# Storing outputs after the last load, moving weight loads, and transposing three more chunks by DMA in a fused recurrence and feed-forward kernel

## The chip, the core and the metric

One core of one Trainium2 chip. The metric is device microseconds of one execution. "Before" is the kernel that was tuned already; "after" is the changed one. A run is called slow when it lies over 1.5% above the fastest run of the same kernel, and ratios use the other runs alone.

## The reference

```python
f = 1 / (1 + exp(-f_logit))                    # q, k, v, f_logit: 4 x 8 x 768 x 48, float32
for t in range(768):
    state = f[:, :, t, :, None] * state + k[:, :, t] (outer) v[:, :, t]
    y[:, :, t] = q[:, :, t] @ state
x = y as 3072 tokens x 384
out = relu(x @ w_in) ** 2 @ w_out              # w_in 384 x 2048, w_out 2048 x 384
```

## The kernel before

The recurrence is worked in 24 chunks of 128 steps, 6 for each of the 4 batch entries; a chunk's result goes through the feed-forward part. A scheduler written in the kernel takes steps with planned durations and makes one static order for each engine. So TensorE, VectorE, ScalarE, GpSimd and SyncE each do their work in a fixed order, and wait in it. The parts that matter:

```python
LOADS = [0, "i0", 1, "i1", 2, "i2", 3, "i3", 4, "o0", "o1", 5, "o2", "o3"] + list(range(6, NCH))
XBAR = 14                                       # from this chunk on, DMA transposes q and k
...
def load(i):                                    # SyncE: f, k, q, v of chunk i, 192 KB each, 192-byte rows
    plan.add(f"{n}{i}", "SP", 0.45, fn, take=["io_" + n], rank=0, data=(1.07, 1024))
...
def load_w(kind, s, behind):                    # GpSimd: a quarter of w_in (i) or w_out (o), cast to bf16
    plan.add(f"cw{kind}{s}", "POOL", 1.0, fn, after=[f"vc.{behind}"], rank=-1, data=(2.4, 0))
for x in LOADS:
    if isinstance(x, int):
        load(x); chunk = x
    else:
        load_w(x[0], x[1], max(chunk - 1, 0))   # waits for the cast of v of that chunk
...
# a chunk: a1 (ScalarE, needs f) -> p1 (TensorE, prefix sum) -> exp -> v1k, v1q (VectorE, need k and q)
#   -> p2 (TensorE: 8 transposes, 4 need k, 4 need q), or one DMA transpose from chunk XBAR on
#   -> p3 -> p4 (needs v, the state); p5 -> s1 -> s2 (GpSimd: the next state)
...
soft = i < NCH - 6
def dma(i=i, soft=soft):                        # the store of a chunk's output
    (nc.gpsimd if soft else nc.sync).dma_start(out[i * C:(i + 1) * C, :], st["ob", i])
```

Fill matmuls on zeros are put where the scheduler expects TensorE to be idle in the first 40 us.

Of the kernel before, what the change touches and what calls it, by code (L numbers as in the profile page):

```python
# [9 lines left out]
F32 = mybir.dt.float32  # L10
# [12 lines left out]
class Planner:  # L23
# [27 lines left out]
    def order(self, fill=None, first=0.0, last=0.0, unit=0.11):  # L51
# [28 lines left out]
        moved_to, queue = 0.0, []  # L80
        while count < len(left):
            while gives and gives[0][0] <= t + 1e-9:
                given.add(heapq.heappop(gives)[1])
            moved = True
            while moved:
                moved = False
                for eng in list(ready):
                    group = ready[eng]
                    if avail.get(eng, 0.0) > t + 1e-9 or not group:
                        continue  # L90
                    best = None
                    for n, r in group.items():
                        s = left[n]
                        if r > t + 1e-9 or not can(s):
                            continue
                        d = s.ways[eng][0]
                        if any(max(avail.get(e, 0.0), t) + w[0] < t + d - 1e-9 for e, w in s.ways.items() if e != eng):
                            continue
                        key = (s.rank if s.rank is not None else r, seq[n])
                        if best is None or key < best[0]:  # L100
                            best = (key, n)
                    if best is None:
                        continue
                    n = best[1]
                    s = left[n]
                    for e in s.ways:
                        ready[e].pop(n, None)
                    for x in s.take:
                        taken[x].append(n)
                    dur, fn = s.ways[eng]  # L110
                    end = t + dur
                    if s.data:
                        us, size = s.data
                        while sum(z for e, z in queue if e > end) + size > self.RING:
                            end = min(e for e, z in queue if e > end)
                        moved_to = max(moved_to, end + self.FIRST) + us
                        queue.append((moved_to, size))
                    avail[eng] = end
                    ran[n] = (t, end, eng)
                    if fill and eng == "PE":  # L120
                        gap = t - max(busy, first) - 2 * unit
                        if gap > 0 and t < last:
                            res.append(lambda k=int(gap / unit) + 1: fill(k))
                        busy = end
                    res.append(fn)
                    count += 1
                    heapq.heappush(events, end)
                    fin = moved_to + self.RECEIPT if s.data else end + s.land
                    heapq.heappush(events, fin)
                    for x in s.give:  # L130
                        heapq.heappush(gives, (fin, tuple(x.split(":"))))
                    for u in users.get(n, ()):
                        waiting[u] -= 1
                        at = ready_at.setdefault(u, {e: 0.0 for e in left[u].ways})
                        for e in at:
                            at[e] = max(at[e], end if e == eng and s.land == self.LAT else fin)
                            heapq.heappush(events, at[e])
                        if waiting[u] == 0:
                            release(u, at)
                    moved = True  # L140
                    break
            while events and events[0] <= t + 1e-9:
                heapq.heappop(events)
            if count < len(left):
                assert events, ("stuck", [n for e in ready.values() for n in e][:20])
                t = events[0]
# [5 lines left out]
def kernel(  # L152
# [10 lines left out]
    nc = tc.nc  # L163
    B, H, S, D = q.shape
    assert (B, H, S, D) == (4, 8, 768, 48)
    C = 128
# [4 lines left out]
    d_model, d_ff = moe_w_in.shape  # L171
    assert d_model == HD
    KS = d_model // C
    FS = d_ff // C
    NCH = B * NC
    IOB = 7
    HTB = 3
    LOADS = [0, "i0", 1, "i1", 2, "i2", 3, "i3", 4, "o0", "o1", 5, "o2", "o3"] + list(range(6, NCH))
    LOADS = [x if isinstance(x, int) else (x[0], int(x[1])) for x in LOADS]
    FILL = 40.0  # L180
    XBAR = 14
    XBAR2 = 18
    UNITS = [(0, 2), (2, 1), (3, 1), (4, 1), (5, 1)] + [(c, 3) for c in range(6, NCH, 3)]

# [6 lines left out]
    ffp = ctx.enter_context(tc.tile_pool(name="ffp", bufs=2))  # L191
# [4 lines left out]

    plan = Planner()
    plan.buffers(**{"io_" + n: IOB for n in "fkqv"})
    plan.buffers(m=2, tr=1, at0=1, at1=1, h=2, o=1, hr=3, hT=HTB, xT=2, ob=4,
                pz=2, az=4, vz=4, ts=3, am=2, ys=3, ep=2, en=4)  # L200
    st = {}
    copy = {"ACT": nc.scalar.copy, "DVE": nc.vector.tensor_copy}
# [64 lines left out]
    def attention(i):  # L267
        c = i % NC
        last = c == NC - 1
        g, o = divmod(i, GC)  # L270
        rank = (i - 6) / 3
# [64 lines left out]
        def p3():  # L336
# [5 lines left out]
                    nc.tensor.matmul(ps[x][:, pr, :], ts[r, NP + pr, :], ts[r, pr, :], skip_group_check=True)  # L342
            st["at", i] = ps
            st["am", i] = [None, None]
        plan.add(f"p3.{i}", "PE", 0.34, p3, after=[f"v2.{i}"], take=["at0", "at1"], rank=rank)

        def v3(x):
            t = work.tile([C, NP, C], BF16, tag="am%d" % x, name="am%d" % x)
# [5 lines left out]
        def p4():  # L354
# [9 lines left out]
            for n, (o_, w, r) in enumerate(ops):  # L364
                nc.tensor.matmul(o_, w, r, start=(n == 0), stop=(n == len(ops) - 1), skip_group_check=True)  # L365
            st["yp", i] = yp
        plan.add(f"p4.{i}", "PE", 0.38 if c else 0.2, p4, after=[f"v3b.{i}", f"vc.{i}"] + ([f"s2.{i - 1}"] if c else [])
                 + ([] if last else [f"p5.{i}"]),
                 take=["m"], give=[f"am:v3a.{i}", f"ts:v2.{i}"] + [f"vz:vc.{i}"] + ([f"az:v1k.{i}"]), rank=rank)

# [19 lines left out]
        if xbar2:  # L390
            plan.add(f"v6.{i}", "SP", 0.7, t6, after=[f"a3.{i}"] + ([f"v6.{i - 1}"] if o else []),
                     take=["xT"] if o == 0 else [], give=[f"ys:a3.{i}"], rank=-2, data=(0.9, 384))
        else:
# [3 lines left out]
                 take=["xT"] if o == 0 else [], give=[f"tr:p6.{i}"])  # L397
# [20 lines left out]
        def s2():  # L418
            nx = sz[(i + 1) % 2]
            for x in range(2):  # L420
                r = slice(DP * x, DP * x + D)
                nc.gpsimd.tensor_mul(nx[r, :, D * x:D * (x + 1)], st["tm", i][r, :, D * x:D * (x + 1)],  # L422
                                     st["en", i][r, HD:HD + NP].unsqueeze(2).to_broadcast([D, NP, D]))
        plan.add(f"s2.{i}", "POOL", 1.0, s2, after=[f"s1.{i}"] + ([f"p4.{i - 1}"] if c else []), give=[f"en:a2n.{i}"])


    def mm1(c0, n):
# [50 lines left out]
    def mm2(g):  # L478
        cuts = [0, 3, 6, 9, 12, 16]
        for tt in range(GC):  # L480
            i = g * GC + tt
            tag = "h" if g == NG - 1 and tt else "tr" if i > max(XBAR, XBAR2) and i % 2 else "o"
# [12 lines left out]
                         give=[f"hT:h{g * GC}.0"] if p == 4 and tt == GC - 1 else [], rank=g + 1 + (tt * 5 + p) / 15)  # L495

            def ev(e, i=i):
                ob = st["ob", i] = ffp.tile([C, d_model], F32, tag="ob", bufs=4, name="ob")
                copy[e](ob, st["o", i])  # L499

            soft = i < NCH - 6

            def dma(i=i, soft=soft):
                (nc.gpsimd if soft else nc.sync).dma_start(out[i * C:(i + 1) * C, :], st["ob", i])  # L504
            both(f"e{i}", 0.46, 0.37, ev, after=[f"o{i}.4"], take=["ob"], give=[f"{tag}:o{i}.0"])
            plan.add(f"d{i}", "POOL" if soft else "SP", 1.0 if soft else 0.45, dma, after=[f"e{i}"], give=[f"ob:e{i}"], rank=-1, data=(0.6, 0 if soft else 128))

    for i in range(NCH):
        attention(i)
# [46 lines left out]
```

## Time and profile before

| | before |
|---|---|
| median of 4 runs | 192.02 us (191.35 to 192.10) |
| span of the profile | 189.8 us |
| start of the seventh prefix sum (chunk 6) | 50.3 us |
| end of the last matmul | 186.4 us |

The prefix sum of chunk 6 serves as a milestone. It is a single 384-column matmul:

```profile
50.34 0.33 PE L286 MATMUL pc<-pz,ut 128*128 128x384 bf16 x1
```

In the kernel before it parts the stretch in which DMA sets the pace from the one that TensorE fills. Ahead of it and behind it I compare the time that passed with the work: the matmuls counted, times the usual distance of their starts (162 ns for 384 columns, 108 for 256, 56 for 128, 42 for 96 and for the 64-row products of p3, 26 for the small ones, fill not counted). What is left over is called lost. With these distances the stretch from the milestone to the last matmul is 136.1 us for 132.7 us of work, 3.4 us lost. Not all of that is waiting: after the last of p3's matmuls the next matmul starts 149 ns later and not 42, once in each chunk, which is 1.9 us in the 18 chunks.

The kernel before has no long wait on TensorE. The three largest of its waits in the whole span, with the total, the number and the longest of each:

```profile
PE hp L444 <- DVE hr L453: 1.9, 1, 1.9
PE pc L286 <- ACT pz L276: 1.8, 3, 1.0
PE idle L522 <- DVE zero L245: 1.0, 1, 1.0
```

### The profile page before, as it was taken

How to read it: one execution, taken by the hardware profiler on the slowest of the kernel's cores; microseconds unless marked ns; L12 is line 12 of the kernel's file. 1: busy time of each engine (PE TensorE's matmuls, PEld its weight loads, DVE VectorE, ACT ScalarE, POOL GpSimd, SP SyncE). 2: the span in 40 equal slices, each digit the busy share in tenths (PEclk: the TensorE clock that was granted, in tenths of full speed). 3: DMA queues.
4: the chain of work that ended last, by engine and by line, in shares of the span. 5: the costliest groups of instructions: out<-in, count | busy, mean ns of one | idle time of the engine just before them, and what ended most of it. 6: DMA issues, size and time to landing. Idle time of an engine off the chain costs nothing.

```text
span 189.8 us, 4807 instructions
## 1 busy us (share of the span) xinstructions
PE 177.5 (93%) x1845; PEld 120.8 (64%) x1845; DVE 127.6 (67%) x259; ACT 132.8 (70%) x281; POOL 54.8 (29%) x105
## 2 busy tenths in 40 slices
PE   6978689989899999999999999999999999999992
PEld 5867478767676666665656666666565666666551
DVE  5484688668397886999988777777667764343300
ACT  4426479786676469999998986978875787565521
POOL 5451343241224561305324311531324401100000
PEclk9999999999999999999999999999999999999999
DMA  6999899999979999999799999979999762211112
GB/s 122 188 191 206 174 187 153 196 164 191 205 137 221 232 227 201 207 197 159 140 155 194 207 137 241 218 109 215 194 216 177 176 60 64 62 45 41 41 41 83
DMA packets 118646, 30.26 MB, mean 159 GB/s; under 512 B 113408, under 2 KB 117760, under 8 KB 118624
## 3 DMA queue, kind: packets, MB, share of 16 engines
q1 hardware_dynamic: 113760, 23.27, 71.2%
q0 software_dynamic: 4864, 6.69, 16.4%
q8 instruction: 14, 0.23, 0.5%
q14 instruction: 8, 0.07, 0.1%
HBM read 25.17 MB, written 4.72 MB: 157 GB/s over the span
## 4 chain that ended last, share of the span: by engine, by line
PE 75%; ACT 11%; DMA 4%; SPq 3%; DVE 3%; issue 2%
PE op L489 31%; PE hp L444 30%; ACT hr L451 4%; DMA io_f<-in_f_logit_dram 4%; SPq L215 3%; PE at L342 3%; PE yp L365 3%; PE tr L318 2%; ACT hT L458 2%; PE pc L286 2%; PE xp L379 1%; PE ds L405 1%; ACT pz L276 1%; ACT e L275 1%; DVE hr L453 1%
## 5 line engine op out<-in xcount | busy, mean ns | idle before, releaser
L444 PE MATMUL hp<-xT,w_in 128*128 128x384 bf16 (+2 forms) x528 | 78.0, 282 | 2.5 <-DVE hr L453 1.9
L489 PE MATMUL op<-w_out,hT 128*128 128x384 bf16 x384 | 76.2, 326 | 0.3 <-ACT ob L499 0.3
L451 ACT ACTIVATE hr<-hp 128x384 bf16<-128x384 f32 (+1 forms) x100 | 50.5, 509 | 20.0 <-PE hp L444 18.0
L444 PEld LDWEIGHTS <-w_in 128*128 128x128 bf16 x528 | 42.3, 98 | 20.7 <-issue 4.0
L489 PEld LDWEIGHTS <-hT 128*128 128x128 bf16 x384 | 35.1, 98 | 21.8 <-issue 0.4
L460 DVE TENSOR_TENSOR hT<-hr 128x384 bf16<-128x384 bf16 (+1 forms) x75 | 29.7, 400 | 27.7 <-ACT hr L451 26.8
L349 DVE TENSOR_TENSOR am<-at,ut 128x512 bf16<-128x512 f32 x48 | 31.6, 685 | 3.7 <-PE at L342 3.4
L422 POOL TENSOR_TENSOR sz<-tm,en 48x192 bf16<-48x192 f32 x40 | 22.0, 549 | 29.9 <-DVE tm L413 7.2
L458 ACT ACTIVATE hT<-hr 128x384 bf16<-128x384 bf16 (+1 forms) x45 | 24.8, 554 | 1.6 <-DVE hr L453 0.3
L504 POOL DMA_DIRECT2D out_dram<-ob x18 | 10.4, 577 | 47.3 <-ACT ob L499 31.2
L280 POOL CAST vz<-io_v 128x384 bf16<-128x384 f32 x24 | 13.6, 567 | 31.2 <-DMA io_v<-in_v_dram 30.7
L306 DVE TENSOR_TENSOR az<-io_k,ep 128x384 bf16<-128x384 f32 x24 | 14.0, 584 | 8.3 <-ACT ep L296 5.1
L275 ACT ACTIVATE e<-io_f 128x384 f32<-128x384 f32 x24 | 12.5, 520 | 7.7 <-DMA io_f<-in_f_logit_dram 7.7
L499 ACT COPY ob<-op 128x384 f32<-128x384 f32 x18 | 8.6, 478 | 12.8 <-PE op L489 12.7
L296 ACT ACTIVATE ep<-pc 128x384 f32<-128x384 f32 x24 | 11.7, 486 | 5.8 <-PE pc L289 5.4
L310 DVE TENSOR_TENSOR az<-io_q,en 128x384 bf16<-128x384 f32 x24 | 14.7, 614 | 0.0
L276 ACT ACTIVATE pz<-e 128x384 bf16<-128x384 f32 x24 | 12.5, 523 | 0.8
L453 DVE TENSOR_SCALAR hr<-hp 128x384 bf16<-128x384 f32 (+1 forms) x20 | 11.6, 584 | 2.0 <-PE hp L444 1.8
L522 PE MATMUL idle<-zero 128*128 128x128 bf16 x119 | 11.9, 256 | 1.0 <-DVE zero L245 1.0
L302 ACT ACTIVATE en<-pc 128x388 f32<-128x388 f32 (+1 forms) x24 | 11.8, 491 | 0.0
L326 DVE COPY ts<-tr 128x1024 bf16<-128x1024 bf16 x14 | 9.6, 687 | 3.1 <-PE tr L318 2.7
L365 PE MATMUL yp<-vz,am 128*128 128x48 bf16 x192 | 9.5, 184 | 1.3 <-DVE am L349 0.8
(40 smaller groups left out, 149.4 us busy)
## 6 DMA issues: line engine op xcount, KB each, us to landing
io_f<-in_f_logit_dram SPq DMA_DIRECT2D x24, 192.0 KB, 4.5
io_k<-in_k_dram SPq DMA_DIRECT2D x24, 192.0 KB, 4.6
io_q<-in_q_dram SPq DMA_DIRECT2D x24, 192.0 KB, 4.5
io_v<-in_v_dram SPq DMA_DIRECT2D x24, 192.0 KB, 4.5
out_dram<-ob POOLq DMA_DIRECT2D x18, 192.0 KB, 3.5
w_in<-in_moe_w_in_dram POOLq DMA_DIRECT2D x4, 384.0 KB, 7.4
w_out<-in_moe_w_out_dram POOLq DMA_DIRECT2D x4, 384.0 KB, 6.9
out_dram<-ob SPq DMA_DIRECT2D x6, 192.0 KB, 1.9
```

What stands on the lines that cost most here:

```text
L275: nc.scalar.activation(e, st["f", i].rearrange("p h d -> p (h d)"), AFT.Exp, scale=-1.0)
L276: nc.scalar.activation(pz[i % 2][:, :, :D], e.rearrange("p (h d) -> p h d", d=D), AFT.Ln, bias=1.0)
L306: nc.vector.tensor_mul(az[i % 4][:, H:, :D], st["k", i], st["ep", i])
L310: nc.vector.tensor_mul(az[i % 4][:, :H, :D], st["q", i], st["en", i][:, :HD].rearrange("p (h d) -> p h d", d=D))
L349: nc.vector.tensor_mul(t, st["at", i][x], ut4)
L365: nc.tensor.matmul(o_, w, r, start=(n == 0), stop=(n == len(ops) - 1), skip_group_check=True)
L422: nc.gpsimd.tensor_mul(nx[r, :, D * x:D * (x + 1)], st["tm", i][r, :, D * x:D * (x + 1)], st["en", i][r, HD:HD + NP].unsqueeze(2).to_broad ...
L444: nc.tensor.matmul(hp[:, x, :], w_in[:, ks, (f + x) * C:(f + x + 1) * C], xT[:, ks, lo:lo + W], start=(ks == 0), stop=(ks == KS - 1), skip ...
L451: nc.scalar.activation(hr[:, :m, :], st["hp", c0, f][:, :m, :], AFT.Relu)
L458: nc.scalar.activation(st["hT", g][:, f:f + m, lo:lo + W], hr[:, :m, :], AFT.Square)
L460: nc.vector.tensor_mul(st["hT", g][:, f:f + m, lo:lo + W], hr[:, :m, :], hr[:, :m, :])
L489: nc.tensor.matmul(st["o", i], hT[:, fs, tt * C:(tt + 1) * C], w_out[:, fs, :], start=(fs == 0), stop=(fs == FS - 1))
```

## The change

The intent, as the diff shows it: stores shall not compete with loads; more feed-forward work shall be ready early, with all weights in by the time chunk 5 arrives; three more chunks give their transposes to the DMA engines.

```diff
+    LATE = NCH - 1
+    OBB = 20
-    LOADS = [0, "i0", 1, "i1", 2, "i2", 3, "i3", 4, "o0", "o1", 5, "o2", "o3"] + list(range(6, NCH))
+    LOADS = [0, 1, 2, "i0", 3, "i1", "i2", "i3", "o0", "o1", 4, "o2", "o3"] + list(range(5, NCH))
-    XBAR = 14
+    XBAR = 11
@@ the scheduler's model: software DMAs (size 0) no longer wait for the ring
-  while sum(z for e, z in queue if e > end) + size > self.RING:
+  while size and sum(z for e, z in queue if e > end) + size > self.RING:
@@ planned durations: p3 0.34 -> 0.42, p4 0.38 -> 0.37
@@ the next state's write waits for the last reader of that buffer, at batch borders too
-  plan.add(f"s2.{i}", "POOL", 1.0, s2, after=[f"s1.{i}"] + ([f"p4.{i - 1}"] if c else []), ...)
+  plan.add(f"s2.{i}", "POOL", 1.0, s2, after=[f"s1.{i}"] + ([f"p4.{i - 1}"] if i else []), ...)
@@ stores: all on SyncE, behind the issue of the last load; 20 output buffers for 4
-  (nc.gpsimd if soft else nc.sync).dma_start(out[i * C:(i + 1) * C, :], st["ob", i])
+  nc.sync.dma_start(out[i * C:(i + 1) * C, :], st["ob", i])
-  plan.add(f"d{i}", "POOL" if soft else "SP", ..., after=[f"e{i}"], rank=-1, ...)
+  plan.add(f"d{i}", "SP", 0.45, dma, after=[f"e{i}", f"v{LATE}"], rank=1, data=(0.6, 128))
```

The wait for `v{LATE}` is one step of SyncE behind another, which the scheduler takes to be ready when the load is issued: in the profile below the last load is issued at 146.03 us and lands at 148.8, and the first store is issued at 146.62.

With the new LOADS, w_in 0 is issued behind the cast of v of chunk 1; w_in 1, 2, 3 and w_out 0, 1 all behind that of chunk 2; w_out 2, 3 behind that of chunk 3.

More of the change, by code (lines that the diff above doesn't have):

```diff
@@ L198 @@
     plan.buffers(**{"io_" + n: IOB for n in "fkqv"})
-    plan.buffers(m=2, tr=1, at0=1, at1=1, h=2, o=1, hr=3, hT=HTB, xT=2, ob=4,
+    plan.buffers(m=2, tr=1, at0=1, at1=1, h=2, o=1, hr=3, hT=HTB, xT=2, ob=OBB,
                 pz=2, az=4, vz=4, ts=3, am=2, ys=3, ep=2, en=4)
@@ L344, in p3 @@
             st["am", i] = [None, None]
-        plan.add(f"p3.{i}", "PE", 0.34, p3, after=[f"v2.{i}"], take=["at0", "at1"], rank=rank)
+        plan.add(f"p3.{i}", "PE", 0.42, p3, after=[f"v2.{i}"], take=["at0", "at1"], rank=rank)
         def v3(x):
@@ L366, in p4 @@
             st["yp", i] = yp
-        plan.add(f"p4.{i}", "PE", 0.38 if c else 0.2, p4, after=[f"v3b.{i}", f"vc.{i}"] + ([f"s2.{i - 1}"] if c else [])
+        plan.add(f"p4.{i}", "PE", 0.37 if c else 0.2, p4, after=[f"v3b.{i}", f"vc.{i}"] + ([f"s2.{i - 1}"] if c else [])
                  + ([] if last else [f"p5.{i}"]),
@@ L423, in s2 @@
                                      st["en", i][r, HD:HD + NP].unsqueeze(2).to_broadcast([D, NP, D]))
-        plan.add(f"s2.{i}", "POOL", 1.0, s2, after=[f"s1.{i}"] + ([f"p4.{i - 1}"] if c else []), give=[f"en:a2n.{i}"])
+        plan.add(f"s2.{i}", "POOL", 1.0, s2, after=[f"s1.{i}"] + ([f"p4.{i - 1}"] if i else []), give=[f"en:a2n.{i}"])
     def mm1(c0, n):
@@ L497, in ev, with dma @@
             def ev(e, i=i):
-                ob = st["ob", i] = ffp.tile([C, d_model], F32, tag="ob", bufs=4, name="ob")
+                ob = st["ob", i] = ffp.tile([C, d_model], F32, tag="ob", bufs=OBB, name="ob")
                 copy[e](ob, st["o", i])
-            soft = i < NCH - 6
-            def dma(i=i, soft=soft):
-                (nc.gpsimd if soft else nc.sync).dma_start(out[i * C:(i + 1) * C, :], st["ob", i])
+            def dma(i=i):
+                nc.sync.dma_start(out[i * C:(i + 1) * C, :], st["ob", i])
             both(f"e{i}", 0.46, 0.37, ev, after=[f"o{i}.4"], take=["ob"], give=[f"{tag}:o{i}.0"])
-            plan.add(f"d{i}", "POOL" if soft else "SP", 1.0 if soft else 0.45, dma, after=[f"e{i}"], give=[f"ob:e{i}"], rank=-1, data=(0.6, 0 if soft else 128))
+            plan.add(f"d{i}", "SP", 0.45, dma, after=[f"e{i}", f"v{LATE}"], give=[f"ob:e{i}"], rank=1, data=(0.6, 128))
     for i in range(NCH):
```

## The prediction

> **What bounds the kernel now.** I read the page's busy line first, then busy time by stretch, then the DMA queues of the first 50 us alone, then TensorE's waits after 50 us, then the end of the chain.
>
> ```profile
> PE 177.5 (93%) x1845; PEld 120.8 (64%) x1845; DVE 127.6 (67%) x259; ACT 132.8 (70%) x281; POOL 54.8 (29%) x105
> ...
> 33.00:50.00 17.00, 14.77 (x217) 11.56 (x214) 10.85 (x22) 12.75 (x25) 4.09 (x7) 1.00 1.11 183
> 50.00:75.00 25.00, 25.00 (x309) 18.07 (x306) 19.74 (x37) 16.75 (x37) 10.76 (x19) 1.00 1.00 208
> 75.00:100.00 25.00, 24.64 (x261) 15.42 (x260) 23.53 (x50) 23.93 (x57) 7.47 (x15) 1.00 1.05 169
> 100.00:185.00 85.00, 85.00 (x712) 52.30 (x711) 51.41 (x111) 60.42 (x131) 18.50 (x33) 1.00 0.71 136
> ```
>
> The rows of the second view give the stretch, then busy time of TensorE matmul, weight load, VectorE, ScalarE and GpSimd, then granted clock, DMA share and GB/s. TensorE is full from 50 us on. "Full" needs a check, as matmuls overlap (one 384-column matmul is drawn 326 ns long). So I took the spacing of the starts: 162 ns for 384 columns, 56 ns for 128, 42 ns for 96, 25 ns for the small ones. Summed over all 1845 matmuls in these spacings, with the fill matmuls at zero, this gives 160.2 us of real work; matmuls end at 186.4 us, so 26.2 us are waiting or fill. Summed over the stretch from the seventh chunk's prefix-sum matmul (starts 50.34 us) to the end, the work is 133.0 us of 136.1: only 3.1 us lost there. The other 23.1 us are lost in the first 50 us, 119 fill matmuls among them.
>
> The first 50 us, DMA queues alone, then the waits of TensorE after 50 us, then when chunk 6's f was issued and when it landed:
>
> ```profile
> q1 hardware_dynamic: 29718, 5.62, 66.9%
> q0 software_dynamic: 3712, 3.15, 41.3%
> ```
> ```profile
> PE pc L286 <- ACT pz L276: 0.2, 1, 0.2
> PE xp L379 <- ACT ys L373: 0.2, 1, 0.2
> ```
> ```profile
> 38.52 0.61 SPq L215 DMA_DIRECT2D io_f<-in_f_logit_dram  x1
> ...
> 49.04 0.53 ACT L275 ACTIVATE e<-io_f 128x384 f32<-128x384 f32 x1
> ```
> ```profile
> DMA to landing us min/median/max: 4.2/5.7/9.4
> ```
>
> The two queues' packets add to 108% of the 16 engines: the DMAs are full from the start. The packet times say what each byte costs: the 96 loads' 98,304 packets of 192 bytes took 17.4 ns each, 4.45 us of all 16 engines for one chunk of f, k, q, v; the eight weight loads took 20.6 us together. Six chunks and a quarter plus the weights are 6.25 x 4.45 + 20.6 = 48.4 us, and f of chunk 6 lands at 38.5 + 9.4 = 47.9 us. The kernel is therefore bound by DMA until chunk 6 arrives and by TensorE work from then on. The end is one block, with no wait inside:
>
> ```profile
> 178.60 7.81 PE op L489 x48
> 186.41 0.02 issue
> 186.44 0.48 ACT ob L499
> ```
>
> **What the Trainium skill says.** "Perfetto Trace Analysis", Identifying the Most-Contended Engine: matmul busy share is a poor measure because matmuls are pipelined. This trace agrees (326 ns drawn, 162 ns apart), so I count spacings. "TensorE: Matmul & The Clock Gate", Wait — 56ns, not 53.3ns?: columns over 2.4 GHz plus 2.5 ns, 162.5 ns for 384; 48 matmuls in 7.81 us are 162.7. "DMA: Bandwidth & Descriptors", Issuing engines are not separate DMA queues: stores from GpSimd and from SyncE share the 16 engines, so changing the issuer saves issue time alone. The trace agrees in that the queue shares add up to a full engine; what helps here is the time of the stores, not their issuer. Same page, Alternative transpose paths: TensorE transposes into PSUM with an identity, which is what the eight matmuls and the copy per chunk do that a DMA replaces.
>
> **The change, part by part.**
>
> 1. Transposes of chunks 11 to 13 by DMA. Removed: 3 x 8 TensorE transposes at 56 ns, 1.3 us of TensorE in the full stretch, so on the path. Removed too: 3 VectorE copies of 128x1024 at 687 ns, 2.1 us, in 75 to 100 us, where VectorE is 23.5 of 25 us busy and ScalarE 23.9. There my spacing sums show TensorE losing about 1.1 us beyond what it loses in quieter stretches; some 0.5 us of it should come back. Added: 3 DMA transposes. The present ten cost 1024 packets of 256 bytes at 30.4 ns each, 1.95 us of the engines, 3.9 us from issue to landing; three cost 5.8 us of DMA.
>
> 2. Stores. Eighteen issues leave GpSimd (18 x 0.58 = 10.4 us busy, waits of 31.2 + 12.9 us before them); GpSimd is 29% busy and off the path: nothing. Their 10.3 us of engine time (packets of queue 0 that are outputs, 576 of 218 ns and 288 of 136 ns over 16) leave the time of the loads and go behind the last load, where the DMA share is under 0.3. That pays for the added transposes: -10.3 + 5.8. No store begins before 49.4 us, so the early bound doesn't move. The last store is issued and lands as before.
>
> 3. Load order. Chunk loads are issued by SyncE, which waits for nothing before 47 us, so what really changes is when GpSimd issues the weights: w_in after chunk 1 and 2 instead of 0, 0, 1, 2; w_out after chunk 2 and 3 instead of 3 and 4. The bytes ahead of chunk 6 are the same. Worked with 4.45 us a chunk and 2.4 to 2.7 us a weight slice: f of chunk 2 comes earlier (about 12 us for 14.9), f of chunk 4 later (17.8 + 15.1 + 1.1 + 1.2 = 35 for 29.8), f of chunk 5 later (22.3 + 20.6 + 1.1 = 44 for 38.7), all weights by about 37 instead of 46.3, f of chunk 6 still at 47.9. I compared the two kernels' TensorE orders: before the seventh prefix sum there are 103 of the 768 feed-forward matmuls (in units of 384 columns) now and 111 then. So 657 x 0.162 = 106.4 us of these remain, and 24.9 us of attention: 131.3 us against 133.0. The 1.7 us are 1.3 more feed-forward done early and 1.3 fewer transposes, less 0.9 of chunk 5's attention that moved behind. From chunk 6: 50.3 + 131.3 + 3.1 = 184.7 us for the last matmul, against 186.4. From chunk 5: 44 + 2.4 (landing to prefix sum as for chunk 6 now) + 135.5 (its remaining work) + 3.1 = 185.0. Both paths give nearly the same, so the order is balanced against the DMAs.
>
> 4. The state buffer's wait: at three batch borders a GpSimd multiply must wait for the last chunk's output matmuls. It guards the result; GpSimd has slack: 0.
>
> 5. Planned durations of two matmul groups, 20 output buffers: they only move the order, counted above.
>
> Sum: 186.4 to 184.7 or 185.0, less 0.5 for the relief, plus about 0.4 for late transposes (below): 1.4 to 1.8 us. A little more of the early gain may be real, as the five weights now queue together beside the loads and the DMA share was highest (1.20 and 1.15) when weights and loads ran together. I choose 2.0: 192.04 - 2.0 = 190.0 us.
>
> **Rivals.** (a) A wait for DMA transposes takes the place of the removed matmuls. The first moves from behind load 15 to just behind f of chunk 14, while the queue is still full (60 to 90 us: hardware queue 100.9%). My estimate of that f's issue is 77.5 us; the transpose would land at 82 to 83, and TensorE's order reaches it at about 80. This could cost 2 to 3 us: 191 to 193. Against it: SyncE waits some 2.7 us for VectorE ahead of each transpose now, so DMA isn't the late one there. (b) The loads become the bound to the end: per chunk 4.45 + 1.95 of DMA against 6.25 of TensorE; f of chunk 23 would slip, and TensorE wait up to 2 us: 191 to 192. Against it: TensorE shows no DMA wait after 50 us with the stores still in the way. (c) The early reordering is worth more: chunk 6 lands by 45.5 because fuller queues move more; 187.5. (d) The stores are hidden now and hidden then, and only the transposes count: 190.7.
>
> **Range and chances.** (a) and (b) together set the upper end, 191.8; (c) with all of the relief the lower, 188.0. Faster by over 2% needs 188.2 or less, that is (c): 0.13. Slower by over 2% needs 195.9, which asks for a stall in every chunk: 0.03.
>
> **What would show it.** Right: transposes 88 instead of 112, copies 11 instead of 14; f of chunk 6 lands at 47 to 48.5; the seventh prefix sum at 50 to 51 us; TensorE full from there, 134 us to its end; no outputs stored before about 145 us; DMA share near 1 from 145 to 160. Wrong: chunk 6 landing over 1.5 us away from 47.9; TensorE waits after 50 us for a transpose or for f; a DMA in the chain in the second half.

## The result, and the profile after

| | before | after |
|---|---|---|
| median | 192.02 us (191.35 to 192.10, 4 runs) | 191.06 us (190.92 to 194.19, 4 runs) |
| ratio of fast runs | 1 | 0.9955, 95% interval 0.9931 to 0.9978 |

Ratios are the mean time of one kernel's fast runs over that of the other's fast runs of the same rounds, so not quite the ratio of the medians. The change gained 0.5%, about 1 us where I had forecast 2.0. That is inside the range that I gave, but only about half of the size. It then turned out that the changed kernel isn't a kernel of one speed: on four chips (A, B, D and E) its medians were 191.06, 192.04, 196.64 and 191.73 us. The kernel before scatters too, though less: its medians on the five chips were 192.02 to 192.85, its single runs 191.28 to 194.88, those of the changed kernel 190.69 to 197.29.

The first profile of after fell in the slow state (granted clock 0.963). I read it from a later run of the same program, after_fourth, of 191.07 us, which is the recorded median. First the page's busy line, then the stretches shown for before, in the same columns:

```profile
PE 175.0 (92%) x1810; PEld 118.9 (63%) x1810; DVE 126.9 (67%) x262; ACT 129.4 (68%) x275; POOL 44.4 (23%) x87
```
```profile
33.00:50.00 17.00, 14.72 (x176) 11.44 (x174) 10.12 (x21) 9.00 (x18) 2.84 (x6) 0.94 1.21 196
50.00:75.00 25.00, 24.74 (x348) 18.76 (x345) 23.02 (x43) 19.82 (x43) 7.04 (x13) 1.00 1.01 175
75.00:100.00 25.00, 24.93 (x248) 15.84 (x243) 22.08 (x47) 23.52 (x55) 7.18 (x13) 1.00 0.91 162
100.00:185.00 85.00, 85.00 (x713) 52.33 (x712) 50.76 (x111) 59.90 (x130) 12.36 (x22) 1.00 0.73 156
```

In 75 to 100 us, DMA share fell to 0.91 (1.05 before) and VectorE to 22.08 us (23.53): the stores have left the DMA engines, and three chunks' copies VectorE. In 33 to 50 us the granted clock is 0.94, which was 1.00. The two DMA queues in the first 50 us:

```profile
q1 hardware_dynamic: 31343, 5.93, 76.9%
q0 software_dynamic: 3712, 3.15, 40.9%
```

They add to 118% where before they added to 108%: more packets in flight, and somewhat more moved. The end is the same block as before, 0.8 us earlier:

```profile
177.83 7.81 PE op L491 x48
185.64 0.02 issue
185.66 0.48 ACT ob L501
```

TensorE's three largest waits in the whole span, and then all of those after 50 us:

```profile
PE ds L407 <- POOL vz L282: 2.6, 4, 2.0
PE tr L320 <- DVE az L312: 2.3, 3, 0.9
PE pc L288 <- ACT pz L278: 1.7, 3, 1.0
```
```profile
PE pc L288 <- ACT ys L375: 0.3, 1, 0.3
```

The milestone starts here:

```profile
51.24 0.33 PE L288 MATMUL pc<-pz,ut 128*128 128x384 bf16 x1
```

So the second part went as forecast. From the milestone to the last matmul it took 134.4 us for 131.0 us of work. No wait of TensorE for a DMA transpose or a load is in that stretch. The first part did not: the milestone is at 51.2 us, not at 50.3 to 50.6. Two of the waits ahead of it are for loads, for v of chunk 3 (through GpSimd's cast, L282, 2.03 us) and for q of chunk 3 (through VectorE's product, L312, 0.94 us); in the kernel before these two kinds come to 0.3 and 0.4 us. The wait at chunk 4's transposes is of another sort. Its q had landed at 38.3 us, and VectorE took the product only at 40.33 us, behind a step of the feed-forward part:

```profile
39.98 0.42 DVE L462 TENSOR_TENSOR hT<-hr 128x512 bf16<-128x512 bf16 x1 [0.42 <-ACT hr L453]
40.33 0.55 DVE L312 TENSOR_TENSOR az<-io_q,en 128x384 bf16<-128x384 f32 x1
```

TensorE waited 0.91 us for it, then 0.79 for the copy of the transposes and 0.57 for an evicted output. The same three waits, 2.3 us, stand in eight of the ten profiles that share this part of TensorE's order, with q of chunk 4 landed anywhere from 32.3 to 40.4 us: they belong to the order and not to the loads. (From 30 us to the milestone the kernel before has 1.9 us of waits, none for a load of over 0.3.)

### The profile page after: what moved, and what is told of

Its sections match the earlier page's. It is cut to its first block, busy times and chain, and to the rows that moved or that the text cites. A ratio compares the mean times of both kernels' runs of the same rounds, so it can differ in the third digit from the quotient of the medians.

```text
span 192.4 us, 4720 instructions
## 1 busy us (share of the span) xinstructions
PE 177.5 (92%) x1810; PEld 119.9 (62%) x1810; DVE 126.6 (66%) x262; ACT 129.4 (67%) x275; POOL 45.0 (23%) x87
## 4 chain that ended last, share of the span: by engine, by line
PE 70%; DMA 10%; SPq 10%; ACT 3%; DVE 2%; issue 2%
PE op L491 33%; PE hp L446 25%; DMA io_q<-in_q_dram 10%; SPq L217 10%; PE at L344 3%; PE yp L367 3%; PE pc L288 1%; PE tr L320 1%; PE ds L407 1%; PE xp L381 1%; ACT hr L453 1%; ACT ob L501 1%; DVE hr L455 1%; PE pc L291 1%; ACT hT L460 0%
## 5 line engine op out<-in xcount | busy, mean ns | idle before, releaser
L446 PE MATMUL hp<-xT,w_in 128*128 128x384 bf16 (+2 forms) x528 | 79.9, 285 | 0.3 <-DVE xT L386 0.2
L491 PE MATMUL op<-w_out,hT 128*128 128x384 bf16 x384 | 79.6, 332 | 0.6 <-ACT ob L501 0.6
L453 ACT ACTIVATE hr<-hp 128x384 bf16<-128x384 f32 (+1 forms) x102 | 52.0, 512 | 24.5 <-PE hp L446 21.6
L462 DVE TENSOR_TENSOR hT<-hr 128x384 bf16<-128x384 bf16 (+1 forms) x87 | 33.4, 385 | 30.4 <-ACT hr L453 28.9
L351 DVE TENSOR_TENSOR am<-at,ut 128x512 bf16<-128x512 f32 x48 | 31.6, 683 | 2.7 <-PE at L344 2.5
L282 POOL CAST vz<-io_v 128x384 bf16<-128x384 f32 x24 | 13.8, 583 | 38.1 <-DMA io_v<-in_v_dram 37.5
L501 ACT COPY ob<-op 128x384 f32<-128x384 f32 x21 | 10.0, 476 | 17.2 <-PE op L491 17.1
L460 ACT ACTIVATE hT<-hr 128x384 bf16<-128x384 bf16 (+1 forms) x33 | 17.8, 540 | 1.7 <-DVE hr L455 0.8
L312 DVE TENSOR_TENSOR az<-io_q,en 128x384 bf16<-128x384 f32 x24 | 15.2, 631 | 1.5 <-DMA io_q<-in_q_dram 1.4
L415 DVE TENSOR_TENSOR tm<-ds,sz 128x384 f32<-128x384 f32 x16 | 8.8, 550 | 8.4 <-PE ds L407 7.9
L455 DVE TENSOR_SCALAR hr<-hp 128x384 bf16<-128x384 f32 (+1 forms) x18 | 10.3, 574 | 1.7 <-PE hp L446 1.7
L344 PE MATMUL at<-ts 64*128 64x128 bf16 x192 | 10.0, 226 | 0.8 <-DVE ts L328 0.8
L320 PE MATMUL tr<-ident,az 128*128 128x128 bf16 x88 | 7.7, 224 | 3.0 <-DVE az L312 2.4
```

The costliest lines, as they stand in the source:

```text
L282: nc.gpsimd.tensor_copy(vz[i % 4], st["v", i])
L312: nc.vector.tensor_mul(az[i % 4][:, :H, :D], st["q", i], st["en", i][:, :HD].rearrange("p (h d) -> p h d", d=D))
L344: nc.tensor.matmul(ps[x][:, pr, :], ts[r, NP + pr, :], ts[r, pr, :], skip_group_check=True)
L351: nc.vector.tensor_mul(t, st["at", i][x], ut4)
L446: nc.tensor.matmul(hp[:, x, :], w_in[:, ks, (f + x) * C:(f + x + 1) * C], xT[:, ks, lo:lo + W], start=(ks == 0), stop=(ks == KS - 1), skip ...
L453: nc.scalar.activation(hr[:, :m, :], st["hp", c0, f][:, :m, :], AFT.Relu)
```

## The experiments

Two theories at the start. T1: the early part lost, because the weight loads are issued in one bunch and take the DMA engines from q and v of chunk 3 and k, q, v of chunk 4, for which TensorE stands in its order. R1: the second part lost, because the added DMA transposes come late. All sixteen runs are here, in four calls on four chips (B to E; A is that of the result). This table has what each profile shows of the two parts: start of the milestone, from there to the last matmul, the work in it, and what was lost. All are single profiles.

| run | milestone | to the end | work | lost | ratio to before (fast runs) |
|---|---|---|---|---|---|
| before | 50.3 | 136.1 | 132.7 | 3.4 | 1 |
| after, first profile (slow) | 54.5 | 134.2 | 131.0 | 3.2 | 0.9955 |
| after_again, chip B | 54.2 | 134.2 | 131.0 | 3.2 | 0.9955 |
| after_third, chip D | 57.5 | 134.2 | 131.0 | 3.2 | 1.0238 |
| after_fourth, chip E | 51.2 | 134.4 | 131.0 | 3.4 | 0.9931 |
| xbar11_only, B | 50.6 | 136.6 | 131.4 | 5.2 | 1.0022 (wrong result) |
| xbar11_state, C (slow) | 54.9 | 136.3 | 131.4 | 5.0 | 0.9973 |
| xbar14, B (slow) | 57.2 | 137.0 | 132.3 | 4.7 | 1.0158 |
| early_stores, D | 53.0 | 135.9 | 130.7 | 5.2 | 1.0049 |
| old_loads, B | 48.3 | 136.9 | 133.3 | 3.6 | 0.9906 |
| old_loads_b, D | 47.6 | 137.5 | 133.3 | 4.1 | 0.9934 |
| old_loads_xbar14, D | 49.1 | 138.4 | 134.6 | 3.8 | 1.0029 |
| spread_early, C | 53.1 | 134.4 | 131.0 | 3.4 | 0.9971 |
| spread_both, C | 51.8 | 134.2 | 131.0 | 3.2 | 0.9962 |
| fill_wait, C (slow) | 55.4 | 134.3 | 131.0 | 3.3 | 0.9984 |
| spread_late, E | 54.7 | 134.4 | 131.0 | 3.4 | 1.0022 |
| mid_loads, E | 49.1 | 137.0 | 133.3 | 3.6 | 0.9956 |
| mid4, E | 49.4 | 136.2 | 131.7 | 4.5 | 0.9951 |

A caution for the whole section: a new load order or store rule makes the scheduler find another order, so those runs change more than the one line. The spread runs and fill_wait keep the changed kernel's order on TensorE, xbar14 keeps it up to chunk 10; xbar11_only and xbar11_state keep that of the kernel before as far. On chip C there is no run of the changed kernel, so the runs of the second call can be set only against the kernel before.

### First call: which part lost

**after_again.** The changed kernel, unaltered.

> The changed kernel once more, unaltered, for a profile in the fast state (the first fell in the slow one, clock 0.963). Theory T1 (the weights bunched behind chunk 2 hold up k, q, v of chunk 4, TensorE stands in its order before 50 us, and that eats the early gain): time 190.9 to 191.2; q of chunk 4 lands near 41 us as in the slow profile (33.8 in the kernel before), TensorE's largest wait is for it, the seventh prefix sum starts at 51 to 52 us and from there to the last matmul 134 us. Rival R1 (the added DMA transposes, or the loads, cost time in the second half): the seventh prefix sum at 50 to 50.5 us, and more than 135.5 us from there to the last matmul.

Measured: 192.04 us median of 7 (191.04 to 194.61), before 192.61; ratio 0.9955 (0.9891 to 1.0020). The profile is of a run of 193.84 us: milestone 54.2 us, then 134.2 us. T1's largest wait came, 4.6 us, but for q of chunk 3 (landed at 26.9 us), not of chunk 4, and milestone and time lie beyond T1's figures. R1's second half did not come.

**xbar11_only.** The kernel before, one number changed.

```diff
-    XBAR = 14
+    XBAR = 11
```

> The kernel before with XBAR 14 -> 11 alone; TensorE's order is the same as before up to chunk 11. T1: the transposes pay all they were predicted to, 1.3 us of TensorE and about 0.5 of relief: 190.0 to 190.5, at least as fast as the whole change. R1: 191.3 to 192.2, since the DMA transposes come late while loads and stores fill the queues.

Measured: 193.04 us, ratio 1.0022 (0.9969 to 1.0076), and a wrong result (relative error 0.043). My first form of T1, that the transposes pay 1.8 us by themselves, fell. The work after the milestone is 1.3 us less, as worked out, but 5.2 us are lost there instead of 3.4. R1's mechanism isn't seen either; TensorE's waits after 51 us are for evicted outputs, none for a transpose (one weight load stood 0.3 us for one at 106.9 us, and no matmul was late for it):

```profile
PE op L489 <- ACT ob L499: 0.8, 2, 0.6
PE op L489 <- DVE ob L499: 0.5, 1, 0.5
```

The wrong result suggests that the scheduler, with other chunks to transpose, put a state write ahead of the last reader at a batch border; xbar11_state tests that.

**xbar14.**

```diff
-    XBAR = 11        # in the changed kernel
+    XBAR = 14
```

> The changed kernel with XBAR back at 14; the order is the changed kernel's up to chunk 10. T1: 1.8 us slower than the changed kernel, 192.4 to 193.0, so slower than the kernel before too: load order and stores together cost about 0.9 us. R1: 190.0 to 190.6, faster than the changed kernel.

Measured: 198.29 us median (194.84 to 199.28), ratio of three fast runs 1.0158 (1.0058 to 1.0258). Slower than T1 said and far from R1. Its order up to chunk 10 is that of after, and the early part was the worst of the call (7.3 us wait for q of chunk 3, landed at 30.0 us; milestone at 57.2 us). In the second part it lost 1.5 us more and had 1.3 us more to do. In these stretches (columns as above) VectorE and ScalarE are full, and the DMA engines all but idle:

```profile
90.00:95.00 5.00, 5.00 (x57) 3.17 (x56) 4.94 (x12) 4.97 (x14) 1.51 (x3) 1.00 0.18 25
95.00:100.00 5.00, 4.92 (x61) 3.29 (x58) 5.00 (x10) 4.94 (x13) 2.05 (x4) 1.00 0.27 51
```

SyncE had come to chunk 14's transpose and stood 9.0 us for VectorE's product, and the loads behind it in SyncE's order stood with it. How much of the 1.5 us is the full VectorE and how much the standing loads, this run doesn't tell.

**old_loads.**

```diff
-    LOADS = [0, 1, 2, "i0", 3, "i1", "i2", "i3", "o0", "o1", 4, "o2", "o3"] + list(range(5, NCH))
+    LOADS = [0, "i0", 1, "i1", 2, "i2", 3, "i3", 4, "o0", "o1", 5, "o2", "o3"] + list(range(6, NCH))
```

> The changed kernel with the load order of before. The scheduler makes a new order from it: 25.2 us of TensorE work before the seventh prefix sum for 27.5 in the changed kernel. T1: q of chunk 4 lands by 35 us again, no TensorE wait of several us for it; seventh prefix sum at 49 to 50.3 us; time 190.5 to 192.0. If the new load order is worth what I predicted for it (1.2 to 1.7 us), this one takes 192.2 to 192.7.

Measured: 190.75 us (190.06 to 193.25), ratio 0.9906 (0.9838 to 0.9975), the fastest of the call. q of chunk 4 landed at 31.1 us, no wait of TensorE over 2.9 us (for chunk 2's prefix sum, with 3.4 us of half clock behind it), milestone at 48.3 us. With the new load order 2.3 us more work is done ahead of the milestone, but the milestone comes 2.9 us (after_fourth) to 9.2 us (after_third) later, so the new order looks like a loss. On this chip alone the intervals of the two kernels overlap (after_again's is 0.9891 to 1.0020).

### Second call: bunch, order or clock

In all three of the early tests TensorE's order is after's. The first two move weight issues in GpSimd's order, after scheduling:

```diff
+    MOVES = [("i0", 0), ("i1", 0), ("i2", 1)]                          # spread_early
+    MOVES = [("i0", 0), ("i1", 0), ("i2", 1), ("o0", 3), ("o1", 3)]    # spread_both
```

**spread_early.**

> The changed kernel in its own order, TensorE's included; only three weight loads move on GpSimd: w_in 0 and 1 behind chunk 0's cast and w_in 2 behind chunk 1's, as in the kernel before. T1 (five weight loads issued within 4 us take the DMA engines from q and v of chunk 3 and k, q, v of chunk 4): q of chunk 3 lands at 23 to 25 us instead of 26.9, TensorE's 4.6 us wait for it goes below 1.5 us, no half clock behind it; f of chunk 2 lands 2 to 4 us later; seventh prefix sum at 51 to 52 us instead of 54.2; 0.5% to 1.2% faster than before. If the bunching is not it: no change of the seventh prefix sum, or later because chunk 2 comes later.

Measured: 192.42 us, ratio 0.9971 (0.9905 to 1.0037). q of chunk 3 at 24.8 us; TensorE's waits at q's transposes shrank to 0.9 us at longest; but chunk 2's f (14.8 us) and k (20.1 us) now make TensorE wait, 2.4 and 2.1 us, and the clock falls twice. Milestone at 53.1 us, beyond the 51 to 52 expected.

**spread_both.**

> As spread_early, and w_out 0 and 1 also move, behind chunk 3's cast, as in the kernel before: the weights are then issued as before, but TensorE keeps the changed kernel's order. T1: q of chunk 3 by 25 us and q of chunk 4 by 33 us as in the kernel before, no waits of several us for them; but the feed-forward matmuls that the order puts early may wait for w_out instead: seventh prefix sum at 50.5 to 52.5 us; 0.3% to 1.2% faster than before. If TensorE's order and not the weights' bunching costs the early time: seventh prefix sum still at 53 us or later.

Measured: 192.30 us, ratio 0.9962 (0.9897 to 1.0027); milestone at 51.8 us, q of chunk 3 at 24.7, q of chunk 4 at 32.3 us, in the expected windows. A 5.4 us wait for f of chunk 2 (landed at 17.3 us) took the place of the other, since TensorE's order has only 2.8 us of work ahead of it. The landings follow the bunch, as T1 says. The time followed them only in part: with the weights issued as before and every q early, the milestone is still no earlier than after_fourth's. That the order was made for other landings is my reading of it.

**fill_wait.** Fill matmuls between the fourth and fifth transpose of chunk 3.

```diff
+                if i == 3 and x == NP:
+                    fill(60)
```

> The changed kernel with 60 fill matmuls (3.4 us at full clock) between the fourth and the fifth transpose of chunk 3, where TensorE waits for q. It tells the wait itself from what the idle time does to the clock. If the half clock (0.5 for 6.8 us behind the wait in the profile) is a loss of its own: granted clock 1.0 from 10 us to the end in the profile, seventh prefix sum 1.5 to 3 us earlier than 54.2, time 0.5% to 1.2% below the changed kernel. If the DMAs alone set the early time: prefix sum within 0.7 us of the changed kernel's, although the clock holds.

Measured: 194.42 us, ratio 0.9984 from two fast runs (0.9868 to 1.0101). A miss as a test: in its profile chunk 3's q came at 21.4 us, so there was nothing to fill; the largest waits were 3.1 us for v of chunk 2, which landed at 18.3 us, before the bunch was issued, and 0.9 us at chunk 4's transposes, and the clock fell twice. One timed run at clock 1.0 took 191.4 us. What the half clock costs by itself stays open.

**xbar11_state.** xbar11_only with the state buffer's wait.

```diff
-  ([f"p4.{i - 1}"] if c else [])
+  ([f"p4.{i - 1}"] if i else [])
```

> The kernel before with XBAR 11 and the state buffer's wait, so xbar11_only mended (that one gave wrong results). It should be correct now, which shows that the wait is needed. R1 (with the stores still among the loads, the added DMA transposes come late and TensorE waits): 192.4 to 193.3, no faster than before, waits for transposed operands near chunks 11 to 13 and again at the end of the loads, from the seventh prefix sum to the end 136 to 137.5 us. T1's first form, that the transposes pay 1.8 us by themselves, fell with xbar11_only and would come back only at 190.5.

Measured: correct; fast runs of 192.21 and 192.50 us (two others slow), ratio 0.9973 (0.9879 to 1.0067); 136.3 us after the milestone, 5.0 lost. The wait is needed for the result and cost no time that these runs show. With the stores early the transposes gain nothing that can be told again; TensorE's waits after 56 us are the same 0.8 and 0.5 us for evicted outputs, so the late transposes of R1 did not come. One thing here speaks against T1 as the whole story: this run has TensorE's order and the load order of the kernel before, without any bunch of five, and yet its milestone is at 54.9 us, 4.3 us behind xbar11_only's (k and q of chunk 5 landed at 44.0 and 46.6 us instead of 39.6 and 40.3).

### Third call: stores and transposes, each alone

**after_third.**

> The changed kernel a third time, beside old_loads on one chip, and for a profile at full clock. Its runs so far fall in two groups: granted clock 0.996 or more, 190.9 to 191.1, and lower clock, 191.2 to 193.8. At full clock T1 wants the seventh prefix sum at 51.0 to 51.7 us (50.3 in the kernel before, 50.3 to 50.8 predicted) and 134.2 us from there to the last matmul; at half clock in the first 50 us it comes up to 3 us later.

Measured: 196.64 us (196.51 to 197.29, 5 runs), ratio 1.0238 (1.0202 to 1.0275). All five count as fast, since a run is measured against the fastest of its kernel on the same chip. The profile has T1's wait at its longest, and again 134.2 us after the milestone. GpSimd issued five weight loads in 3.9 us:

```profile
16.48 2.35 POOL L233 DMA_DIRECT2D w_in<-in_moe_w_in_dram  x3
18.82 1.52 POOL L235 DMA_DIRECT2D w_out<-in_moe_w_out_dram  x2
```

From 12 to 34 us the queues' shares were these, in after_third and then in the kernel before (the order of the lines is by share):

```profile
q0 software_dynamic: 2656, 2.36, 71.0%
q1 hardware_dynamic: 8388, 1.58, 46.9%
```
```profile
q0 software_dynamic: 2055, 1.83, 54.0%
q1 hardware_dynamic: 11361, 2.15, 53.3%
```

q of chunk 3, issued at 15.1 us, took this long to land (in the kernel before the same load, issued at 20.6, took 4.4 us and landed 5 us earlier):

```profile
DMA to landing us min/median/max: 14.8/14.8/14.8
```

TensorE did the four transposes that need k and stood for the four that need q:

```profile
22.77 0.39 PE L320 MATMUL tr<-ident,az 128*128 128x128 bf16 x4
30.64 0.61 PE L320 MATMUL tr<-ident,az 128*128 128x128 bf16 x4 [7.48 <-DVE az L312]
31.04 0.31 PE L522 MATMUL idle<-zero 128*128 128x128 bf16 x1
31.15 2.75 PE L446 MATMUL hp<-xT,w_in 128*128 128x256 bf16 x18
```

The last line is 18 matmuls in 2.75 us, where after_fourth's took 1.49 us at the same place. The clock records have 0.5 from 26.9 to 33.8 us, and again from 47.4 to 50.8. In the page's row of forty slices it shows as two dips:

```profile
PEclk9999975998799999999999999999999999999998
```

**old_loads_b.**

> old_loads again, for the difference to the changed kernel on one chip. T1: 0.3% to 0.8% faster than the changed kernel (0.9906 to 0.9955 so far, on a chip that scattered). If the load order is no loss after all: within 0.2% of it.

Measured: 191.15 us (190.45 to 193.38), ratio 0.9934 (0.9893 to 0.9974). The difference to the changed kernel was 3%, more than the 0.3% to 0.8% that I gave, because of after_third's long wait. Here the intervals lie far apart, so on this chip the new load order is a loss; the sign is T1's on both chips.

**old_loads_xbar14.** old_loads with XBAR 14: late stores without the added transposes.

> The kernel before with the stores behind the loads, 20 buffers, the state wait and the planned durations, but XBAR 14 and the old load order: old_loads less its transposes. If stores and transposes are complements (the store's room in the DMA engines is what the transposes need): this is 1.3 to 2 us slower than old_loads, 191.8 to 192.8, about as the kernel before, since the stores alone free no TensorE work. If the late stores alone give the gain: within 0.4 us of old_loads.

Measured: 192.97 us (192.31 to 195.69), ratio 1.0029 (0.9988 to 1.0070), 1.8 us over old_loads_b. As expected of complements (parts that pay only together): its interval lies wholly above that of old_loads_b.

**early_stores.** The changed kernel with the stores as before.

```diff
-  plan.add(f"d{i}", "SP", 0.45, dma, after=[f"e{i}", f"v{LATE}"], rank=1, ...)
+  plan.add(f"d{i}", "POOL" if soft else "SP", ..., after=[f"e{i}"], rank=-1, ...)
```

> The changed kernel with its stores as in the kernel before (18 on GpSimd as soon as each is ready). If complements: TensorE loses 1 to 2 us more from the seventh prefix sum to the end (4.5 to 5.5 beyond its work, as in xbar11_only's 5.2, for 3.2), time 1 to 2 us above the changed kernel. If the stores don't matter: within 0.4 us of it and 3.0 to 3.6 us lost there.

Measured: 193.54 us (192.94 to 198.84), ratio 1.0049 (1.0003 to 1.0095); 5.2 us lost after the milestone, as expected of complements. The comparison of its whole time with after's is void on this chip, where the long wait of after_third ruled. Its waits after the milestone are 0.9 us in two for outputs that ScalarE evicted and 0.3 us for a prefix sum; none for a DMA transpose.

The runs make a square, all against the kernel before: neither, 1; late stores alone 1.0029; transposes alone 1.0022 (0.9973 with the state's wait); both, with the old load order, 0.9906 and 0.9934. What makes the two complements isn't shown. A 256-byte packet of a DMA transpose took 31.7 ns in xbar11_only and 29.3 in early_stores, against 23.2 to 24.5 in the four profiles of after and 26.2 in old_loads, so early stores and transposes do slow each other; but no matmul waited visibly for a transpose, and moving the stores also changes GpSimd's order and the scheduler's.

### Fourth call: is there an order without the loss

The prediction's cause was open still, as after_third had shown how far its time can go.

**spread_late.** TensorE's order as in after; w_out 0 and 1 behind chunk 3's cast.

```diff
+    MOVES = [("o0", 3), ("o1", 3)]
```

> The changed kernel in its own order, w_out 0 and 1 issued behind chunk 3's cast instead of chunk 2's: a bunch of three weight loads beside q and v of chunk 3 instead of five. T1: q of chunk 3 lands by 26 us wherever it came at 26.9 or 29.9 with the bunch of five, TensorE's wait for it falls below 4 us, and the time follows it (0.5% to 2% below the changed kernel where that one has the long wait; the same where it hasn't). If the bunch is not the cause: q of chunk 3 and the wait unchanged.

Measured: 193.50 us, ratio 1.0022 (0.9907 to 1.0137). With three loads in the bunch q of chunk 3 landed at 23.3 us. But after_fourth on this chip had it at 22.9 with five, so the comparison doesn't tell the bunch of three from that of five here. The wait moved to the other side: TensorE's order wants w_out early, and its longest wait became that one:

```profile
PE op L493 <- DMA w_out<-in_moe_w_out_dram: 3.7, 1, 3.7
```

So the order asks for the weights and for chunk 4 at the same time; whichever the DMA engines bring later is waited for.

**after_fourth.**

> The changed kernel a fourth time, beside its mended versions on one chip. T1: from the seventh prefix sum to the last matmul 134.2 us again, whatever the early part does; its time is 136.8 us (134.2 and the end of 2.6) plus the start of that prefix sum, plus 2.7 for what the time has beyond the span, within 1 us.

Measured: 191.73 us median of 4 (190.69 to 196.17), ratio 0.9931 (0.9825 to 1.0037). The profiled run took 191.07 us with the milestone at 51.2 us and 134.4 us after it. My rule gives 190.7 (51.2 + 136.8 + 2.7), 0.4 us off; its two constants were both wrong and made up for each other (3.6 us from the last matmul to the end of the span, not 2.6, and 1.8 us beyond the span, not 2.7).

**mid_loads** and **mid4.**

```diff
+    LOADS = [0, 1, "i0", 2, "i1", 3, "i2", "i3", 4, "o0", "o1", 5, "o2", "o3"] + ...         # mid_loads
+    LOADS = [0, "i0", 1, "i1", 2, "i2", 3, "i3", "o0", 4, "o1", "o2", 5, "o3"] + ...         # mid4
```

> The changed kernel with a load order between: w_in 0 behind chunk 0, 1 behind chunk 1, 2 and 3 behind chunk 2, w_out two each behind chunks 3 and 4, so never more than two weight loads together. If T1 is the whole matter of the early time: no wait of over 2.5 us on TensorE, seventh prefix sum at 47.5 to 49 us with 25.2 us of work before it, 189.8 to 190.9, 0.5% to 1.2% below the kernel before.

> The changed kernel with the old load order but w_out 0 one chunk earlier, which lets the scheduler put 26.8 us of work before the seventh prefix sum (25.2 in old_loads, 27.5 in the changed kernel). T1 and the sum: seventh prefix sum at 48.5 to 50 us, 189.5 to 190.7. If it starves chunk 4 as the bunch of five does: a TensorE wait of over 3 us and 191 or more.

Measured: mid_loads 191.78 us (190.76 to 192.74), ratio 0.9956 (0.9847 to 1.0065), milestone at 49.1 us, longest wait 2.4 us. mid4 192.13 us (191.05 to 194.66), ratio 0.9951 (0.9844 to 1.0058), milestone at 49.4 us, longest wait of TensorE 1.6 us, 4.5 us lost after it. (mid4 also has w_out 2 a chunk earlier, which the expectation doesn't say.) Both do without the long wait, as T1 says, and kept the clock at 1.0 up to the last work, but both times are over what was expected. Neither is told from after_fourth on this scattered chip, and neither beat old_loads' ratios. Of all versions, old_loads is the one whose ratio lay below 1 with its whole interval on two chips.

## Why the prediction was wrong, point by point

**What bounds the kernel: right before the change, not after it.** From the milestone on TensorE lost 3.2 to 3.4 us in all four profiles of after, as forecast. But DMA until chunk 6 no longer sets the milestone. f of chunk 6 landed at 45.7 us in after_fourth, 2.2 us before the forecast, which is one of the signs of being wrong that I had named (47.0 to 47.4 in the other three), and the milestone came 5.5 us later, for 2.4 in the kernel before. Rival (c) had its condition almost met (45.5 us), and its gain did not come.

**Step 1, transposes: right in its terms, but for their condition.** 88 transposes remained and 11 copies; the work after the milestone fell from 132.7 to 131.0 us, the 1.7 us that I had summed (1.3 of it the transposes). Between the 13th and 17th prefix sum, the stretch of full VectorE and ScalarE, TensorE's lag behind its work grew by 1.4 us before and by 0.9 in after_again, the 0.5 us of relief that I gave (xbar14, in the changed kernel's order up to chunk 10, has 1.4). It was no net gain: from the 7th to the 13th prefix sum the lag grew by 0.9 to 1.1 us in the profiles of after and by 0.6 before. What I did not see: the same transposes gain nothing while the stores are early (5.0 to 5.2 us lost instead of 3.4). I counted the stores' room in the DMA engines but put no time on it.

**Rivals (a) and (b), late transposes or loads in the second part: wrong in all four profiles of after**, and so was the 0.4 us that I charged for them. In xbar11_only and early_stores the visible waits were for evicted outputs, about 1 us of the additional 1.8. What brought those evictions late isn't settled, as the orders differ.

**Step 3, the early part: this is the step that failed.** It said that the seventh prefix sum would start at 50.3 us (50.6 by chunk 5's path), because f of chunk 6 would land at 47.9 as before, and I then took off another 0.2 to 0.6 us because fuller queues move more. (The sum of that passage is 1.5 to 1.8 us; it prints 1.4. And its reason, that DMA share was highest with weights and loads together, 1.20 and 1.15, was misread: the same view has 1.23 from 40 to 45 us and 1.27 from 130 to 135.) The profile of a fast run has the milestone at 51.2 us; others have 54.2 and 57.5. In the sum: the milestone 0.9 us later, work 1.7 us less, lost 0.0, together 0.8 us; the end of the last matmul moved from 186.4 to 185.6 us. The term for the milestone was forecast as 0 to 0.3, less what I took off. Of the 0.9 us, 0.4 is more work ahead of the milestone (27.5 us for 27.1) and 0.5 more time lost there (23.7 us for 23.2). These are single profiles: that of before is of a run of 191.61 us, 0.4 below its median, and after the last matmul the span goes on for 3.6 us where it was 3.4, so the two profiled runs differ by 0.5 us and the medians by 1.0.

The landings of f that this step worked out were nearly right: chunk 4 at 35 us (34.4 measured), chunk 5 at 44 (41.8), chunk 6 at 47.9 (45.7, for the fuller queues did move more). The error was to follow f alone. I asked when each chunk could begin, and not when TensorE, in its order, would meet the first matmul that needs q or v. In after_fourth v of chunk 3 landed at 30.1 us and TensorE stood 2.0 us for it, at this line of its timeline:

```profile
30.75 0.33 PE L407 MATMUL ds<-vz,az 128*128 128x96 bf16 x4 [2.03 <-POOL vz L282]
```

Behind it the clock was halved for 3.4 us, and then came the order's own three waits of 2.3 us, the last of them over at 44.8 us. From there to the milestone TensorE had no wait of over 0.15 us and worked off what was left. An early chunk 6 is then no help: nobody waits for it.

**What I had no rival for: the time depends on how the two queues share the engines.** q of chunk 3 landed at 21.5, 26.9, 29.9 and 22.9 us in the four profiles of one program. Where chunk 2's v lands at about 16 us, the bunch falls on chunk 3; in the first profile it landed at 18.3 us, the bunch went out 2 us later, and chunk 4's q came at 41.2 us instead. In that profile the longest wait, 3.1 us, was for chunk 2's v itself, ahead of the bunch. Over all eighteen profiles q of chunk 3 landed between 21.4 and 30.0 us in the seven with the bunch of five, and between 22.8 and 25.0 in the eleven without it: the bunch scatters this landing, rather than delays it each time. In a fixed order each late landing is a wait. How the 0.5 us of after_fourth divides between the loads, the clock and the order stays open, as no run changed one of them alone at its timing.

**And the clock.** The waits of TensorE came with stretches of granted clock 0.5: 6.8 us from near the end of the 4.6 us wait of after_again, 6.8 and 3.4 us in after_third (the first from 3.7 us into the 7.48 us wait), 3.4 us in after_fourth. "TensorE: Matmul & The Clock Gate", What's actually happening, describes it as a gate that halves the clock after an idle window of about 3.4 us; the lengths here are multiples of 3.4 us, which agrees. So a wait can cost twice, once by itself and once in the matmuls behind it (18 matmuls took 2.75 us instead of 1.49). How much of the whole early loss is the clock is not settled; fill_wait missed its wait.

**The stores and the state buffer.** Moving the stores cost next to nothing at the end, as forecast (3.6 us from the last matmul to the end of the span, for 3.4). They went out from 146.6 us on in after_fourth (about 145 forecast):

```profile
146.62 3.25 SPq L504 DMA_DIRECT2D out_dram<-ob  x6
```

The state's wait was rightly put at zero, and xbar11_only against xbar11_state shows that the result depends on it.

## What to carry to other kernels

When a change reorders loads whose bytes stay the same, follow the operand that each in-order engine meets first, not just the operand that starts a chunk; a bunch of large transfers on one queue can hold a small one on another for 15 us. Test such a change on more than one chip or with many runs: four medians of this program span 191.1 to 196.6 us, and the gain in view was 1 us. And try the parts of a change in a square: here late stores alone and DMA transposes alone gained nothing that the runs could tell, both together 0.7% to 0.9%, and the third part, the load order, gave some of it back.

## What the Trainium skill lacked or had wrong

- "DMA: Bandwidth & Descriptors", Issuing engines are not separate DMA queues, has the queues interleave on the same 16 engines (and elsewhere take turns packet by packet), but no figure for how unequal that can be, nor that it varies from execution to execution. With five weight loads queued by GpSimd (1024- and 768-byte packets) the software queue took 71.0% of the engines and the loads of 192-byte rows 46.9% (packet times overlap), and one 192 KB load took 14.8 us instead of 4.4; the same load landed at 21.5, 22.9, 26.9 and 29.9 us in four profiles of one program.
- "TensorE: Matmul & The Clock Gate", What's actually happening, gives an idle window of about 3.4 us as what halves the clock, and its Why this matters for your kernels section advises against idle gaps of over about 3 us. In after_fourth the clock fell to 0.5 from 31.6 to 35.0 us although the longest wait there was 2.03 us; taken alone, the advice is too lenient for a stretch with several short waits. The 3.4 us steps agree (3.4, 6.8, 10.2 us in thirteen of the eighteen profiles). I cut each run from 5 us to its last matmul into these steps, in phase with its falls, and summed the matmuls' usual distances, fill counted. The full-clock step just ahead of each of the 17 falls held 0 to 0.37 of work; none of the 904 others, which held 0.40 or more, was followed by a fall. So in these runs the step before a fall was mostly idle, not wholly, and a fall depends on how the waits lie in the steps.
- "DMA: Bandwidth & Descriptors", Latency and other measured facts, has a bandwidth for DMA transposes, but not what one costs beside loads and stores: here 1024 packets of 256 bytes took 30.4 ns each, 1.95 us of all 16 engines for 262,144 bytes, in before (134 GB/s, worked out from these), and 23.2 to 24.5 ns in the four profiles of the changed kernel, where no store was issued before the last load.
